# Output weights split again in the second pass, pieces kept for two units, and forms moved to another SBUF offset

## The chip, the cores and the metric

The kernel runs on one core of a Trainium2 chip. The metric is the device time of one execution in microseconds. The profile is one separate execution with the hardware profiler on; it has a time of its own.

## The reference

Inputs: q, k, v of 4 batches x 8 heads x 576 positions x 64; four expert weights w1 (512 x 1024) and w2 (1024 x 512); a dense layer w_in (512 x 2048) and w_out (2048 x 512), which arrive as float64. Everything is computed in float32.

```python
q_s = softmax(q, axis=-1);  k_s = softmax(k, axis=positions)
kv  = einsum('bhsd,bhse->bhde', k_s, v)
x   = einsum('bhsd,bhde->bhse', q_s, kv)        # -> 2304 tokens x 512
p   = domain_probs / (domain_probs.sum(-1) + 1e-9)
y   = sum_e p[:, e] * (relu(x @ w1[e]) @ w2[e]) # 4 experts, 1024 wide
h   = y @ w_in;  out = (h / (1 + exp(-1.702 h))) @ w_out   # 2048 wide
```

## The kernel before, in words

**Precision.** Each large matmul is done in three products of 32-bit "float32r" parts: an operand is split into a high part (a copy on ScalarE, ACT, that rounds) and a low part (the rest, by a subtraction). High x high, high x low and low x high are summed in PSUM.

**Tiling.** The 2304 tokens are three groups, each of two equal halves: group 0 (2 x 512), group 1 (2 x 256) and group 2 (2 x 384). The two layers (experts: "moe", then dense: "ffn") are cut into units of 256 hidden columns: 16 for moe, 8 for ffn. A unit's first product (`mm1`, L842) uses Strassen's seven block products, six matmuls each, so 42 matmuls a step, whose moving operands are the "forms": blocks b11, b21, b12, b22 of x and their sums t1 to t4, each with a high and a low tile (`blocks`, L575). A 512-wide matmul reads 512 columns of a form. The second product (`mm2`, L936) is a 128-token tile at a time, six matmuls of 512 columns: stationary the hidden activations h_hi and h_lo, moving the output weights W2.

**Passes.** SBUF does not hold the forms of all groups, so each layer is passed over twice: first pass with group 0 (one step a unit), second pass with groups 1 and 2 (two steps a unit). In the moe layer the first 3 units (AHEAD) are run before the Strassen forms are there, as plain halves of group 0: steps "L" of units 0, 1, 2 and then "R" of units 0, 1, 2, four products of six matmuls each (`turns`, L674). Each of those six has an index m of its own, 0 to 5 (NPLAIN); `insts` lists all indices.

**Weights.** For each m the pieces of w1 (tag "w1", ring of 10 tiles) and of w2 (tag "w2", ring of 4, halves w20 and w21 of 512 KB with high and low part) are made from raw tiles (`load_w`, ring of 3): a copy on ACT (`hi_w1`, `hi_w2`) and a subtraction on GpSimd (POOL) (`lo_w1`, `lo_w2`). What comes again later is stored to DRAM (`store_part`, L707, in the start through `first_stores`) and read back then in place of being made (`new_part`, L692; `again`, L688). That holds for w1 pieces and w2 halves alike.

**Order.** All engine queues are in order, and the order is the program's. The start (`START`, L1114) is written out by hand: attention of batches 0 and 1 and steps 0 to 5. From step 6 a planner `step` (L1067) issues five stages a step: matmuls and evictions as `STAGES` (L923) says, then the pieces of the next unit's w1 (`prepare`), then w2 (stages 1 and 3, L1098), loads, one deferred transposition to the next layer's input, and some background "turns" (`pump`). In stage 1 stand the rest of the previous step's output tiles (REST), in stage 4 the first half of the next (TILES). The background is first the attention of batches 2 and 3 (`attend2`, L406, two turns a stage; the list of turns is at L543, an empty string is a turn with nothing; a new head enters each eight turns), then the decoding of float64 weights (`decode`, L792, 1.25 turns a stage: five VectorE instructions and more, one on POOL, for each of 32 tiles).

**Lines that the change touches.** `kg`/`kgm` (L483) transpose a column maximum on TensorE and make a diagonal `dg` on VectorE (DVE); `ks` (L489) multiplies it on TensorE, `ksv` subtracts. `xf` (L533) copies an attention result out of PSUM on ACT into `xo` and `put_x` (L633) sends it to DRAM from the SyncE (SP) queue. `to_x2` (L649) transposes a finished moe tile, copies it to `xt` (on DVE where the ffn layer runs already, else on ACT) and sends it from ACT; `xo` and `xt` share a ring of two. `total` (L955) adds a tile into `acc`; the first unit of a pass writes it, for ffn by a copy on ACT. `edge` (L1149) is a tile at the top end of SBUF that nothing reads; the forms of groups 0 and 2 lie below it. With 56 elements all of these tiles begin at 1792 modulo 2048 bytes of a partition; W2, raw tiles, h_hi and h_lo, `acc` and group 1's forms begin at 288 modulo 2048 (w1's pieces too).

Of the kernel before, what the change touches and what calls it, by code (L numbers as in the profile page):

```python
# [8 lines left out]
F32 = mybir.dt.float32  # L9
# [13 lines left out]
def tile_linear_attention_moe_gelu(  # L23
# [32 lines left out]
    P = 128  # L56
# [349 lines left out]
    def attend2(b, j, c0, nc_, keys, live):  # L406
# [109 lines left out]
        def group(g):  # L516
            def t(_):
                y["qT", g] = t_("qT", [P, W])
                y["t", g] = bk(f"t{g}", [P, W])
                for c in range(GS):  # L520
                    T.transpose(
                        y["t", g][:, c * SP : (c + 1) * SP],
                        y["qn"][:, g * GS + c].rearrange("p h d -> p (h d)"), ident[:SP, :SP],
                    )

            def qT(_):
                A.copy(y["qT", g], y["t", g])

            def px(_):
                y["px", g] = bk(f"px{g}", [P, W])  # L530
                T.matmul(y["px", g], kvbd[:, j, :], y["qT", g], start=True, stop=True)  # L531

            def xf(eng):  # L533
                put_x(j, b * S + (c0 + g * GS) * SP, W, y["px", g], A, None)

            for fn in (t, qT, px, xf):
                ops[fn.__name__ + str(g)] = fn
# [288 lines left out]

    acc = {}
    x2 = []  # L830
    def mm(ps, w, x, start, stop):
        (wh, wl), (xh, xl) = w, x
# [9 lines left out]
    def mm1(g, i, m, ho):  # L842
# [92 lines left out]

    def mm2(g, i, lt, m, ho):  # L936

        kind, e, f, pas, first, last = units[g]
# [6 lines left out]
        def product(_=None):  # L945
            y["ps"] = ps = pools["pso", "p"].tile([P, DM], F32, tag="o", name=f"po{g}_{ti}")
            n = 0
            for ft in range(FT):
                hh, hl = h_hi[:, ft, s], h_lo[:, ft, s]
                wh, wl = W2[m, ft]  # L950
                for a, b in ((hh, wh), (hh, wl), (hl, wh)):
                    T.matmul(ps, a, b, start=(n == 0), stop=(n == 3 * FT - 1))  # L952
                    n += 1

        def total(_=None):  # L955
            ps = y["ps"]
# [110 lines left out]
    def step(k_, tiles, before):  # L1067
# [61 lines left out]
        Lb21u:b0@V oa21:1 Lb21v:b0@V a2:s0 rc:2 c2:s0 km:1_0 ra:s0 la21:2@G a2:s1 km:1_2 rc:s0 ra:6 kg:1_0 la:s0 c2:s1  # L1129
        ra:s1 kgm:1_0 kg:1_2 lc:s0 rc:s1 ow21:1 la:s1 kgm:1_2 y0:s0 kdg:1_2 y1:s0 lc:s1 z0:s0 kdg:1_0 k:1_1 z1:s0  # L1130
        oa21:2 +s1:6 ks:1_0 q:1_0 ks:1_2 ksv:1_0 y2:s0 q:1_2 km:1_1 +s3:6 ke:1_0 +s2:6 q:1_1 y3:s0 z2:s0 +s4:6 ksv:1_2
        y1:s1 z3:s0 v:1_3 qm:1_0 ke:1_2 qm:1_2 oa11:0 z1:s1 qs:1_0@G pk:1_2 qm:1_1 oa11:1 qs:1_2@G qe:1_0 pk:1_0
        oa22:1 rz:1_2 rr:1_2 bd0:1_2 bd1:1_2@A qu:1_0 qs:1_1@G oa12:1 ha12:2 kg:1_1 qe:1_2 y0:s1 rz:1_0 kgm:1_1 rr:1_0
        q:1_3 ha22:2 bd0:1_0 qu:1_2 la12:2@G bd1:1_0@A qe:1_1 pk:1_3 ow20:0 la22:2@G z0:s1 qu:1_1 qp:1_2 qp:1_0 qr:1_2
        rc:6 qr:1_0 qn:1_2@G rz:1_3 qm:1_3 a1:s2 rr:1_3 bd0:1_3 c1:s2 bd1:1_3@A kdg:1_1 qp:1_1 oa12:0 qs:1_3@V t1:1_2
        qT1:1_2@A qr:1_1 ow21:0 qe:1_3 ks:1_1 a2:s2 ksv:1_1 qn:1_1@G ra:s2 px1:1_2 la:s2 ke:1_1 oa22:2 xf1:1_2@V
        t0:1_2 pk:1_1 qu:1_3 oa11:2 qT0:1_2@V ow20:1 wh0:2 t0:1_1 qp:1_3 qn:1_0@V px0:1_2 wh1:2 qT0:1_1@A qr:1_3
        wl1:2@G rz:1_1 xf0:1_2@A rr:1_1 c2:s2 bd1:1_1@V rc:s2 oa21:0 bd0:1_1 lc:s2 t1:1_0 qn:1_3@G t0:1_0 qT1:1_0@A
        px0:1_1 oa12:2 qT0:1_0@A px1:1_0 xf0:1_1@V px0:1_0 xf1:1_0@A wl0:2@V t0:1_3 xf0:1_0@V qT0:1_3@A ha11:3 t1:1_3
        t1:1_1 qT1:1_3@V px0:1_3 ha21:3 qT1:1_1@V px1:1_3 xf0:1_3@V ha12:3 px1:1_1 xf1:1_3@A y2:s1 xf1:1_1@V ow21:2  # L1140
        open Hb12:b0 y3:s1 z2:s1 Lb12:b0@V ha22:3 y0:s2 ow20:2 z3:s1 Hb22:b0 y1:s2 z0:s2 Lb22:b0@V wh0:3 wh1:3 ha11:4
        y2:s2 z1:s2 y3:s2 z2:s2 ha21:4 z3:s2 a1:s3 c1:s3 St1:b0@V Ht1:b0 ha12:4 ha22:4 a2:s3 Lt1:b0@G c2:s3 ra:s3
        la:s3 rc:s3 St2:b0@V lc:s3 wh0:4 wh1:4 ha11:5 ha21:5 a1:s4 c1:s4 Ht2:b0 y0:s3 y1:s3 Lt2:b0@G z0:s3 y2:s3 z1:s3
        a2:s4 ra:s4 la:s4 c2:s4 rc:s4 lc:s4 y3:s3 z2:s3 z3:s3 ha11:6 hs4:6 la11:6@V ls4:6@G ha12:5 ha22:5 wh0:5 wh1:5
        a1:s5 c1:s5 St3:b0@V Ht3:b0 y0:s4 a2:s5 ha22:6 la22:6@G y1:s4 z0:s4 ra:s5 Lt3:b0@V la:s5 z1:s4 c2:s5 rc:s5
        lc:s5 y2:s4 ha12:6 hs2:6 la12:6@V y3:s4 z2:s4 hs3:6 ls2:6@V z3:s4 ls3:6@V hs1:6 ls1:6@G St4:b0@G
# [32 lines left out]
    for m in range(NSTART + 1):  # L1179
# [97 lines left out]
```

## Time and profile before

| | us |
|---|---|
| median of 3 runs | 1230.19 (1230.03 to 1230.43) |
| the profiled execution's own time | 1235.11 |
| its span, first to last instruction | 1233.3 |
| TensorE (PE) matmul busy | 1209.0 (98%) |
| DVE busy | 850.4 (69%) |
| ACT busy | 464.7 (38%) |
| POOL busy | 358.7 (29%) |
| DMA | 225.86 MB, 16 engines busy about 56% |

PE is busy nearly everywhere, but matmuls overlap: a 512-column matmul is shown with 0.39 us and the next starts 0.23 us later. So PE's time is read from start to start, or from how long a run of matmuls takes in the chain of work, and not from its busy share. The granted clock is full (2.4 GHz) but for two short stretches, mean 0.995.

### The profile page before, as it was taken

What the parts mean: (1) busy time and instruction counts of PE and PEld (TensorE: products, weight loads), DVE (VectorE), ACT (ScalarE), POOL (GpSimd) and SP (SyncE); (2) the same over time, 40 slices, a digit from 0 to 9 for tenths busy, and PEclk for the clock granted to TensorE, in tenths of its full rate; (3) what the DMA queues carried; (4) which work ended last, traced back from release to release, by engine and by line L of the source; (5) the groups of instructions that cost most, each with busy time, mean ns of one, the idle gap of its engine ahead of it and who ended that gap; (6) DMA issues with size and microseconds to landing.
All of it is one profiled execution on the core that took longest, in us unless ns stands there. A gap on an engine that the chain in (4) does not pass through costs nothing.

```text
span 1233.3 us, 17497 instructions
## 1 busy us (share of the span) xinstructions
PE 1209.0 (98%) x6276; PEld 1043.9 (85%) x6276; DVE 850.4 (69%) x1416; ACT 464.7 (38%) x1010; POOL 358.7 (29%) x389
## 2 busy tenths in 40 slices
PE   8999899999999999999999999999999999999998
PEld 7878688887888899899899889898788889899997
DVE  7875778767567759998999975577355774454554
ACT  5544345433434352222122222145645544333332
POOL 4424657554553001111112331025454500000000
PEclk9999899999999999999999999999999999999999
DMA  8884966664566366666566632535655655334323
GB/s 199 250 303 141 324 210 203 204 230 149 198 217 226 105 198 213 212 209 211 194 194 221 202 110 69 196 121 186 232 203 213 228 170 161 111 107 122 108 92 86
DMA packets 134423, 225.86 MB, mean 183 GB/s; under 512 B 30400, under 2 KB 62144, under 8 KB 133696
## 3 DMA queue, kind: packets, MB, share of 16 engines
q1 hardware_dynamic: 124832, 220.02, 55.2%
q10 hardware_dynamic: 9504, 4.72, 1.3%
q8 instruction: 50, 0.82, 0.3%
q14 instruction: 37, 0.30, 0.1%
HBM read 137.40 MB, written 87.29 MB: 182 GB/s over the span
## 4 chain that ended last, share of the span: by engine, by line
PE 86%; DVE 9%; DMA 4%; ACT 1%; issue 1%; SPq 0%; POOL 0%; ACTq 0%; DVEq 0%
PE po L952 43%; PE px L836 21%; PE pz L836 10%; PE py L836 5%; DVE acc L964 2%; DVE h_lo L885 2%; DMA w64o<-in_moe_w_out 1%; PE pk L506 1%; PE p L378 1%; DMA x_ffn<-xt 1%; PE ca_R L836 1%; PE cc_R L836 1%; DMA q<-in_q 1%; DVE dso L803 1%; PE px L531 1%
## 5 line engine op out<-in xcount | busy, mean ns | idle before, releaser
L952 PE MATMUL po<-w,h_hi 128*128 128x512 f32 x1728 | 538.4, 393 | 2.4 <-DVE xt L110 2.0
L952 PEld LDWEIGHTS po<-w,h_hi 128*128 128x128 f32 x1728 | 320.8, 189 | 65.2 <-DVE xt L110 2.9
L952 PE MATMUL po<-w,h_lo 128*128 128x512 f32 x864 | 337.7, 391 | 3.2 <-DVE h_lo L885 3.2
L964 DVE SCALAR_TENSOR_TENSOR acc<-po,pr,acc 128x512 f32<-128x512 f32 x270 | 194.6, 745 | 70.1 <-PE po L952 69.7
L952 PEld LDWEIGHTS po<-w,h_lo 128*128 128x128 f32 x864 | 162.8, 188 | 39.4 <-DVE h_lo L885 4.5
L110 ACT COPY u<-px 128x384 f32<-128x384 f32 (+2 forms) x138 | 65.3, 473 | 237.7 <-PE px L836 230.3
L973 DVE TENSOR_TENSOR acc<-po,acc 128x512 f32<-128x512 f32 x126 | 85.7, 689 | 58.5 <-PE po L952 57.4
L866 DVE TENSOR_TENSOR u<-pz,u 128x384 f32<-128x384 f32 (+2 forms) x138 | 75.4, 546 | 52.9 <-ACT u L110 52.1
L774 POOL TENSOR_TENSOR s<-s,s 128x256 fp32r<-128x256 f32 x94 | 80.1, 860 | 74.2 <-ACT s L768 59.7
L787 POOL TENSOR_TENSOR w<-rc,w 128x512 fp32r<-128x512 f32 x46 | 60.4, 1314 | 86.6 <-ACT w L781 71.2
L774 POOL TENSOR_TENSOR a<-ra,a 128x256 fp32r<-128x256 f32 x69 | 53.4, 774 | 90.0 <-ACT a L768 80.0
L879 ACT ACTIVATE h_hi<-px 128x256 fp32r<-128x256 f32 (+2 forms) x45 | 21.8, 484 | 144.3 <-PE px L836 144.2
L885 DVE SCALAR_TENSOR_TENSOR h_lo<-u,h_hi 128x256 fp32r<-128x256 f32 (+2 forms) x90 | 63.7, 732 | 12.5 <-ACT h_hi L879 12.3
L823 POOL TENSOR_TENSOR doi<-doi,dti 128x512 f32<-128x512 f32 x16 | 21.0, 1312 | 161.1 <-DVE doi L820 155.0
L762 POOL TENSOR_TENSOR s<-ra 128x256 f32<-128x256 f32 x48 | 40.5, 844 | 75.8 <-DMA ra<-wi 49.8
L866 DVE TENSOR_TENSOR p<-py,p 128x384 f32<-128x384 f32 (+2 forms) x69 | 37.8, 548 | 33.6 <-PE py L836 30.1
L781 ACT CAST w<-rc 128x512 fp32r<-128x512 f32 x48 | 29.6, 620 | 72.2 <-PE po L952 71.5
L879 ACT ACTIVATE h_hi<-u 128x256 fp32r<-128x256 f32 (+2 forms) x90 | 46.3, 515 | 16.0 <-DVE u L866 16.0
L823 POOL TENSOR_TENSOR doo<-doo,dto 128x512 f32<-128x512 f32 x16 | 21.3, 1330 | 103.7 <-DVE doo L820 91.6
L110 ACT COPY p<-px 128x384 f32<-128x384 f32 (+2 forms) x69 | 32.9, 477 | 37.7 <-PE px L836 37.5
L768 ACT CAST s<-s 128x256 fp32r<-128x256 f32 x96 | 36.8, 404 | 24.0 <-POOL s L762 17.1
L889 DVE TENSOR_TENSOR h_lo<-sc,h_hi 128x512 fp32r<-128x512 f32 (+2 forms) x24 | 13.4, 559 | 44.3 <-ACT h_hi L881 44.3
(312 smaller groups left out, 2470.2 us busy)
## 6 DMA issues: line engine op xcount, KB each, us to landing
w<-k_w SPq DMA_DIRECT2D x54, 512.0 KB, 4.5
k_w<-w SPq DMA_DIRECT2D x48, 512.0 KB, 5.1
a<-k_a SPq DMA_DIRECT2D x84, 256.0 KB, 2.8
k_s<-s SPq DMA_DIRECT2D x84, 256.0 KB, 5.2
s<-k_s SPq DMA_DIRECT2D x84, 256.0 KB, 3.3
k_a<-a SPq DMA_DIRECT2D x75, 256.0 KB, 5.2
ra<-in_moe_w SPq DMA_DIRECT2D x19, 512.0 KB, 4.3
rc<-in_moe_w SPq DMA_DIRECT2D x16, 512.0 KB, 6.1
```

Source lines behind the costliest of these rows:

```text
L110: (eng.copy if eng is A else eng.tensor_copy)(o, i)
L762: G.tensor_tensor(out=o, in0=block_w(m, l), in1=block_w(m, r), op=op)
L774: eng.tensor_tensor(out=lo, in0=block_w(m, x), in1=hi.bitcast(F32), op=ALU.subtract)
L787: eng.tensor_tensor(out=lo, in0=raw[m, 1][:, c, :], in1=hi.bitcast(F32), op=ALU.subtract)
L823: G.tensor_tensor(out=o, in0=o, in1=t.bitcast(F32), op=ALU.add)
L836: T.matmul(ps, a[:, kk, :], b[:, kk, :], start=(start and n == 0), stop=(stop and n == 5), skip_group_check=True,)
L866: return lambda _: V.tensor_tensor(out=y[o], in0=y[ps], in1=y[o], op=ALU.add)
L879: A.activation(hi, y[c], AF.Relu)
L885: V.scalar_tensor_tensor(out=lo, in0=y[c], scalar=0.0, in1=hi.bitcast(F32), op0=ALU.max, op1=ALU.subtract)
L952: T.matmul(ps, a, b, start=(n == 0), stop=(n == 3 * FT - 1))
L964: V.scalar_tensor_tensor(out=acc[ti], in0=ps, scalar=pe, in1=acc[ti], op0=ALU.mult, op1=ALU.add)
L973: V.tensor_tensor(out=acc[ti], in0=ps, in1=acc[ti], op=ALU.add)
```

## The change

1. **W2 in the second passes.** Halves of w2 are no longer stored and read back; in the second pass they are loaded raw and split again (ACT copy, POOL subtraction). Only unit 0's, at m = 5, come from DRAM. In `step` they are made in stages 2 and 3, not 1 and 3.
2. **Two units held.** The R halves run in the order 1, 2, 0. Units 1 and 2 use the w1 and w2 pieces of their L halves (`HOME`: m = 3 uses m = 1's, m = 4 uses m = 2's). What the first unit of a tile is, is told by a set `begun`. `START` loses their loads and some stores, and gets m = 5's loads earlier.
3. **Queues.** Attention results of batches 2 and 3 are sent from ACT's queue. `xt` is always copied on ACT; ffn's first `acc` is copied on DVE.
4. **Turns.** One more empty turn before `ks ksv` in `attend2`.
5. **`edge`** has 432 elements: the forms of groups 0 and 2 lie 1504 bytes lower, at 288 modulo 2048.

```diff
-                put_x(j, b * S + (c0 + g * GS) * SP, W, y["px", g], A, None)
+                put_x(j, b * S + (c0 + g * GS) * SP, W, y["px", g], A, None, A)
...
-        turns = ["km", "qm qs", "", "", "kg kgm", "qe", "", "ks ksv", "qu qn", "ke", "", "", "pk", "", "bd"]
+        turns = ["km", "qm qs", "", "", "kg kgm", "qe", "", "", "ks ksv", "qu qn", "ke", "", "", "pk", "", "bd"]
...
-                S_.dma_start(out=x_d["moe", i][:, j, d - g0 : d - g0 + m], in_=o[:, d - t0 : d - t0 + m])
+                by.dma_start(out=x_d["moe", i][:, j, d - g0 : d - g0 + m], in_=o[:, d - t0 : d - t0 + m])
...
-            copy(V if stage[1] else A, o, pt.rearrange("p k t -> p (k t)"))
+            copy(A, o, pt.rearrange("p k t -> p (k t)"))
...
-    turns = [(g, "L") for g in range(AHEAD)] + [(g, "R") for g in range(AHEAD)]
+    turns = [(g, "L") for g in range(AHEAD)] + [(g, "R") for g in (*range(1, AHEAD), 0)]
+    HOME = {AHEAD + n: 1 + n for n in range(AHEAD - 1)}
...
-        names = (PLAIN if m < NPLAIN else STRASSEN) + ("w20", "w21")
+        if m in HOME:
+            continue
+        names = PLAIN if m < NPLAIN else STRASSEN
         again.update({(m, x): (u, x) in had for x in names})
+        again.update({(m, x): m == NPLAIN - 1 for x in ("w20", "w21")})
...
-                    mm(y["c" + x], W1[m, f"a{ft + 1}{kh + 1}"], X[0, b], kh == 0, kh == 1)
+                    mm(y["c" + x], W1[HOME.get(m, m), f"a{ft + 1}{kh + 1}"], X[0, b], kh == 0, kh == 1)
...
-                wh, wl = W2[m, ft]
+                wh, wl = W2[HOME.get(m, m), ft]
...
+            first = (kind, ti) not in begun
+            begun.add((kind, ti))
...
             if first:
-                A.copy(acc[ti], ps)
+                V.tensor_copy(acc[ti], ps)
...
-                if s in (1, 3) and (m, s // 2) not in W2:
-                    hi_w2(m, s // 2)
-                    lo_w2(m, s // 2, G)
+                if s in (2, 3) and (m, s - 2) not in W2:
+                    hi_w2(m, s - 2)
+                    lo_w2(m, s - 2, G)
...
-    pools["edge", "p"].tile([P, 56], F32, name="edge")
+    pools["edge", "p"].tile([P, 432], F32, name="edge")
```

## Rows read from the trace of the kernel before

**Rows 1.** The page, part 4: the chain that ended last, by engine.

```profile
PE 86%; DVE 9%; DMA 4%; ACT 1%; issue 1%; SPq 0%; POOL 0%; ACTq 0%; DVEq 0%
```

**Rows 2.** The chain in order of time: start us, us, what.

```profile
137.03 8.00 PE po L952 x24
...
295.77 4.34 PE px L836 x12
...
334.84 5.46 PE po L952 x24
340.30 2.80 PE px L836 x12
```

**Rows 3.** Timeline of PE, second pass: start us, us, instruction (first of six each).

```profile
464.43 0.34 PE L836 MATMUL px<-t3hmoe,s 128*128 128x384 f32 x1
...
465.47 0.28 PE L836 MATMUL px<-b11hmoe,a 128*128 128x256 f32 x1
...
466.18 0.28 PE L836 MATMUL py<-b21hmoe,a 128*128 128x256 f32 x1
```

**Rows 4.** Waits of PE: who waited for whom, us, times, longest us.

```profile
PE pb L491 <- DVE dg L487: 4.7, 1, 4.7
PE po L952 <- DVE h_lo L885: 3.2, 2, 1.6
PE po L952 <- DVE xt L110: 2.0, 1, 2.0
PE pk L506 <- DVE acc L964: 1.7, 1, 1.7
...
PE pz L836 <- DVE u L866: 1.2, 1, 1.2
```

**Rows 5.** Stretches: us, busy by engine (instructions), granted clock, DMA share, GB/s.

```profile
136.60:142.20 5.60, 5.60 (x15) 4.44 (x15) 4.60 (x6) 3.02 (x8) 5.60 (x7) 0.50 1.02 390
...
500.00:550.00 50.00, 50.00 (x275) 45.06 (x275) 48.62 (x91) 11.19 (x27) 7.88 (x6) 1.00 0.66 202
550.00:600.00 50.00, 50.00 (x279) 45.04 (x277) 44.65 (x84) 10.55 (x26) 6.60 (x6) 1.00 0.65 210
600.00:650.00 50.00, 48.45 (x269) 43.79 (x269) 48.35 (x91) 10.89 (x27) 9.31 (x7) 1.00 0.59 195
650.00:700.00 50.00, 50.00 (x278) 45.18 (x277) 46.76 (x85) 12.45 (x32) 12.66 (x12) 1.00 0.64 211
700.00:745.00 45.00, 42.21 (x235) 37.83 (x234) 35.98 (x58) 11.03 (x29) 15.48 (x17) 1.00 0.35 117
```

**Rows 6.** Timeline of DVE: start us, us, instruction, [idle before].

```profile
134.30 1.93 DVE L487 TENSOR_SCALAR dg<-ident,gm 128x128 f32<-128x128 f32 x1
...
285.81 7.04 DVE L885 SCALAR_TENSOR_TENSOR h_lo<-u,h_hi 128x512 fp32r<-128x512 f32 x1 [0.27 <-ACT h_hi L879]
...
571.58 1.32 DVE L803 TENSOR_SCALAR dsi<-w64i 128x512 int32<-128x512 int32 x1
...
583.90 0.43 DVE L803 TENSOR_SCALAR dso<-w64o 128x512 int32<-128x512 int32 x1 [3.96 <-DMA w64o<-in_moe_w_out]
...
869.33 0.69 DVE L110 COPY xt<-pt 128x512 f32<-128x512 f32 x1 [3.72 <-DMA x_ffn<-xt]
```

**Rows 7.** Timeline of POOL: first and last of the eight that run on end.

```profile
285.07 1.79 POOL L466 TENSOR_TENSOR qn<-q,qu 96x768 f32<-96x768 f32 x1 [0.55 <-DVE qu L462]
...
291.56 0.74 POOL L774 TENSOR_TENSOR s<-s,s 128x256 fp32r<-128x256 f32 x1
```

**Rows 8.** The page, part 5: the two instructions that make a half of W2.

```profile
L787 POOL TENSOR_TENSOR w<-rc,w 128x512 fp32r<-128x512 f32 x46 | 60.4, 1314 | 86.6 <-ACT w L781 71.2
...
L781 ACT CAST w<-rc 128x512 fp32r<-128x512 f32 x48 | 29.6, 620 | 72.2 <-PE po L952 71.5
```

**Rows 9.** The page, part 6: DMA issues, count, KB each, us to landing.

```profile
w<-k_w SPq DMA_DIRECT2D x54, 512.0 KB, 4.5
```

**Rows 10.** Waits of the SP queue at the sending of attention results.

```profile
SPq L646 <- ACT xo L110: 49.3, 11, 12.9
```

More of the change, by code (lines that the diff above doesn't have):

```diff
@@ L631, in forms, with put_x @@
         then()
-    def put_x(j, t0, w, src, eng, first):
+    def put_x(j, t0, w, src, eng, first, by=S_):
         d, o = t0, None
@@ L723, in put_away @@
             stores.pop(0)[1]()
-    stage = [0, False]
+    stage = [0]
     def put_old():
@@ L825, in decode @@
         yield
-    acc = {}
+    acc, begun = {}, set()
     x2 = []
@@ L936, in mm2 @@
     def mm2(g, i, lt, m, ho):
-        kind, e, f, pas, first, last = units[g]
+        kind, e, f, pas, _, last = units[g]
         t0, n = SPANS[i]
@@ L1073, in step @@
         ops = mm1(g, i, m, places[k_])
-        stage[1] = units[g][0] == "ffn"
         st = STAGES[units[g][0]] if k_ + 1 < len(steps) else LAST
@@ L1128, in tile_linear_attention_moe_gelu @@
         px0:0_3 c1:s1 wl1:1@V xf0:0_3@A k:1_0 Hb21u:b0 a1:s1 ha11:2 la22:1@V a1:s0 Hb21v:b0 k:1_2 la11:2@V ha21:2
[L1129 to L1146, printed above, removed]
+        Lb21u:b0@V Lb21v:b0@V a2:s0 rc:2 c2:s0 km:1_0 ra:s0 la21:2@G a2:s1 km:1_2 rc:s0 ra:6 kg:1_0 la:s0 c2:s1 ra:s1
@@ new lines, in tile_linear_attention_moe_gelu @@
+        kgm:1_0 kg:1_2 lc:s0 rc:s1 la:s1 kgm:1_2 y0:s0 kdg:1_2 y1:s0 lc:s1 z0:s0 kdg:1_0 k:1_1 z1:s0 +s1:6 ks:1_0
+        q:1_0 ks:1_2 ksv:1_0 y2:s0 q:1_2 km:1_1 +s3:6 ke:1_0 +s2:6 q:1_1 y3:s0 z2:s0 +s4:6 ksv:1_2 y1:s1 z3:s0 v:1_3
+        qm:1_0 ke:1_2 qm:1_2 oa11:0 z1:s1 qs:1_0@G pk:1_2 qm:1_1 oa11:1 qs:1_2@G qe:1_0 pk:1_0 oa22:1 rz:1_2 rr:1_2
+        bd0:1_2 bd1:1_2@A qu:1_0 qs:1_1@G oa12:1 ha12:2 kg:1_1 qe:1_2 y0:s1 rz:1_0 kgm:1_1 rr:1_0 q:1_3 ha22:2 bd0:1_0
+        qu:1_2 la12:2@G bd1:1_0@A qe:1_1 pk:1_3 ow20:0 la22:2@G z0:s1 qu:1_1 qp:1_2 qp:1_0 qr:1_2 rc:6 qr:1_0 qn:1_2@G
@@ new lines, in tile_linear_attention_moe_gelu @@
+        rz:1_3 qm:1_3 a1:s2 rr:1_3 bd0:1_3 c1:s2 bd1:1_3@A kdg:1_1 qp:1_1 oa12:0 qs:1_3@V t1:1_2 qT1:1_2@A qr:1_1
+        ow21:0 qe:1_3 ks:1_1 a2:s2 ksv:1_1 qn:1_1@G ra:s2 px1:1_2 la:s2 ke:1_1 oa22:2 xf1:1_2@V t0:1_2 pk:1_1 qu:1_3
+        oa11:2 qT0:1_2@V wh0:2 t0:1_1 qp:1_3 qn:1_0@V px0:1_2 wh1:2 qT0:1_1@A qr:1_3 wl1:2@G rz:1_1 xf0:1_2@A rr:1_1
+        c2:s2 bd1:1_1@V rc:s2 oa21:0 bd0:1_1 lc:s2 t1:1_0 qn:1_3@G t0:1_0 qT1:1_0@A px0:1_1 oa12:2 qT0:1_0@A px1:1_0
+        xf0:1_1@V px0:1_0 xf1:1_0@A wl0:2@V t0:1_3 xf0:1_0@V qT0:1_3@A t1:1_3 t1:1_1 qT1:1_3@V px0:1_3 qT1:1_1@V
@@ new lines, in tile_linear_attention_moe_gelu @@
+        px1:1_3 xf0:1_3@V px1:1_1 xf1:1_3@A y2:s1 xf1:1_1@V ha11:5 ha21:5 open Hb12:b0 y3:s1 z2:s1 Lb12:b0@V y0:s2
+        z3:s1 Hb22:b0 y1:s2 z0:s2 Lb22:b0@V y2:s2 z1:s2 y3:s2 z2:s2 z3:s2 a1:s3 c1:s3 St1:b0@V Ht1:b0 a2:s3 Lt1:b0@G
+        c2:s3 ha12:5 ha22:5 ra:s3 la:s3 rc:s3 St2:b0@V lc:s3 a1:s4 c1:s4 Ht2:b0 y0:s3 y1:s3 Lt2:b0@G z0:s3 y2:s3 z1:s3
+        a2:s4 ra:s4 la:s4 c2:s4 rc:s4 lc:s4 y3:s3 z2:s3 z3:s3 wh0:5 wh1:5 ha11:6 hs4:6 la11:6@V ls4:6@G a1:s5 c1:s5
+        St3:b0@V Ht3:b0 y0:s4 a2:s5 ha22:6 la22:6@G y1:s4 z0:s4 ra:s5 Lt3:b0@V la:s5 z1:s4 c2:s5 rc:s5 lc:s5 y2:s4
@@ L1147, in tile_linear_attention_moe_gelu @@
+        ha12:6 hs2:6 la12:6@V y3:s4 z2:s4 hs3:6 ls2:6@V z3:s4 ls3:6@V hs1:6 ls1:6@G St4:b0@G
     """
     open_pool("edge", bufs=1, side="right")
-    pools["edge", "p"].tile([P, 56], F32, name="edge")
+    pools["edge", "p"].tile([P, 432], F32, name="edge")
     open_pool("xp0", bufs=2, side="right")
@@ L1185, in tile_linear_attention_moe_gelu @@
             new["l" + x] = lambda e, m=m, x=x: lo_w1(m, x, e or G)
-            new["o" + x] = lambda _, m=m, x=x: first_stores.pop((m, x))()
+            new["o" + x] = lambda _, m=m, x=x: first_stores.pop((m, x), lambda: None)()
         for c in range(FT):
@@ L1189, in tile_linear_attention_moe_gelu @@
             new[f"wl{c}"] = lambda e, m=m, c=c: lo_w2(m, c, e or G)
-            new[f"ow2{c}"] = lambda _, m=m, c=c: first_stores.pop((m, f"w2{c}"))()
+            new[f"ow2{c}"] = lambda _, m=m, c=c: first_stores.pop((m, f"w2{c}"), lambda: None)()
         add(m, new)
```

## The prediction

> **What bounds the kernel now.** I read the chain of waits first: 86% of it is PE [rows 1]. So the time is PE's matmuls, one after the other, plus the few places where PE stands still, and an edit counts only by what it does to one of the two. Work taken off DMA, ACT, POOL or SP is worth nothing by itself.
>
> The second view is the rate of the matmuls. 24 of 512 columns whose moving operand is W2 take 5.46 us, 227.5 ns each; 12 with a form of group 0 take 2.80 us, 233.3 ns each [rows 2]. In the second pass six forms of 384 columns take 1.04 us (173.3 ns each) and six of 256 take 0.71 us (118.3) [rows 3]. 128 columns more are 55 ns, so 512 should be some 228: W2's matmuls keep to that line and group 0's forms lie 5.8 ns above it.
>
> The third is PE's waits. In the body of the kernel they are five: 4.7 for `dg`, 1.7 for `acc` before a `pk`, 3.2 for h_lo in two places, 1.2 for `u`, 2.0 for `xt` [rows 4]. All name DVE, though DVE is busy only 69% over the span: the average hides stretches in which it is full. Two of the stalls cost twice, since the clock falls behind them. After the first the granted clock is 0.50, the 1.2 GHz level, for some 5 us [rows 5], and 24 matmuls take 8.00 us for 5.46; after the second 12 take 4.34 for 2.80 [rows 2]. Before both falls PE had stood.
>
> Behind these stalls is POOL. While eight POOL instructions run on end from 285.07 to 292.30 [rows 7], one DVE subtraction of two SBUF operands, begun at 285.81, ends at 292.85: of the 7.04 us for two of them nearly 6 are waiting [rows 6]. `dg` has 1.93 us for a 128x128 scaling; a decode step shows 1.32 and the same operation elsewhere 0.43 [rows 6]. So POOL work is not free: it can hold DVE, and DVE holds PE.
>
> The Trainium skill ("SBUF — State Buffer", section "SBUF: two separate sides") says that GpSimd and a VectorE instruction with two SBUF inputs take a port in turn, the loser blocked for the other's whole instruction. The row agrees on the blocking, but 6 us is longer than any one POOL instruction: DVE did not get in between two. By the rule a POOL subtraction more costs DVE at most 1.3 us; by the row a whole run of them. By the rule the slower rival below could cost a step 1.3 us at most, and the sum would stand.
>
> **The change part by part.**
>
> *Forms at 288.* Six steps of 24 matmuls, and 13 + 8 first-pass steps of 42, use 512-column forms: 144 + 882 = 1026. At 5.8 ns each that is 5.9 us. W2 lies at 288 and runs on the lower line in 2592 matmuls; group 0's forms lie at 1792 and don't. What speaks against the offset as cause is that group 2's 384-column forms lie at 1792 too and show nothing. Bounds: 0 to -5.9; a loss is excluded, as W2's matmuls already show how an operand at 288 runs. I take -5.5, some of the 144 lying beside attention's chains in the start.
>
> A rule of the Trainium skill speaks against it: the same page and section says that PE never waits on anyone at its SBUF port, and names no cost of an offset; by it this term would be nil and the sum 5.5 us higher.
>
> *The empty turn before `ks`.* The heads enter every eight turns and two turns make a stage, so `kg` (fifth turn) stays in its stage and `ks` (eighth, now ninth) goes one stage later, for every head. For the first head `ks` stood at the end of stage 3: 12 matmuls (2.8 us) after `kg`, then 4.7 us of waiting. It now comes behind stage 4's 24 output matmuls, 5.5 us more, which cover the wait by 0.8. The wait goes, and the slow clock behind it (8.00 - 5.46 = 2.5 us). Together -7.2. Bounds: 0, if what held DVE comes later too, to -7.2. I take -7.0. Late next is `ke` to `pk`, which loses a stage of distance but keeps one.
>
> *W2 in stages 2 and 3, first passes.* ACT no longer waits for REST before the copy (71.5 us, off PE's path, and POOL waited behind it [rows 8]); but POOL's 1.31 us now stands right before the stage whose h_lo PE needs next. The `pk` stall arose there: 1.7 + 1.5 us of slow clock = 3.2. Bounds: -3.2 (its POOL run is broken up) to +3.2 (a second such place). With nothing to decide between them I take 0.
>
> *W2 made anew in second passes.* Each unit adds two ACT copies of 0.62 and two POOL subtractions of 1.31 us [rows 8] every 26 us. ACT is a quarter busy there. The cost is in the decode, about 450 to 745 us, where DVE is full: 48.6, 44.7, 48.4 and 46.8 of 50 us [rows 5], idle 11.6 us in 200. The trace has a test of more POOL work: with 7.9 busy us in 50 PE loses nothing, with 12.7 neither, with 15.5 in 45 PE is busy only 42.2 [rows 5]. The change adds some 5 us of POOL per 50: the first stretches come to 13, the last, where units 0 to 2 are split too, to 20. DVE loses about half a POOL instruction for each, an estimate from the 0.9 us lost in the row above and none in others: 10 us in 200 against 11.6 idle. On the other side the 54 reads of 512 KB [rows 9], each of which stood on SP until a ring place came free, are mostly gone, so the decode's own loads land sooner: DVE once stood 3.96 us for one, at 580 [rows 6], and PE's loss of 1.55 in the stretch from 600 [rows 5] comes out of that backlog. Bounds: -4.4, if the h_lo and `u` stalls both go; above, 11 units x 2 x 1.31 = 28.8 us of DVE less its idle time at the same share (11.6 x 286/200 = 16.6): +12. I take +3, nearest to what the 15.5 us row cost. After the decode and in ffn DVE is half busy; 0.5 us for short waits, bounds 0 to 1.
>
> *`xt` on ACT, first `acc` on DVE.* The DVE copy waited 3.72 us for an earlier send to land [rows 6], and PE 2.0 behind the next copy. On ACT the same copy would wait for the same landing, now in front of evictions. With no W2 stores beside it the landing should be sooner. Bounds: -2.0 to +2.0; I take -1.
>
> *Sends from ACT, held units, less DMA.* SP stood 49.3 us for `xo` copies [rows 10], and the loads behind them with it; POOL gets its raw weights sooner. Each send costs ACT its issue, and ACT is not among those that PE waits for in the body [rows 4]. About 41 MB less moves (54 + 48 halves less 24 raw loads, and the held pieces), but no DMA is among PE's waits of the body either. I take 0, bounds -1 to +1.
>
> The sum: -5.5 - 7.0 + 0 + 3 + 0.5 - 1 + 0 = -10.0. The profiled execution (1235.11, 1.8 us more than its span) lies 4.9 above the median of the runs; against its own time the sum gives 1225.1, and I carry the difference to the median: 1230.2 - 10 = 1220.
>
> **The rivals.**
>
> *The offset does nothing.* For it: the 384-column forms. Against: 512 columns at 288 and at 1792 differ by the same 5.8 ns throughout. Then -4.5: 1225.7. The skill's rule on PE's port, above, would give this. Chance 0.22.
>
> *The stall moves.* `ks` is covered by only 0.8 us; if DVE or POOL is later by that much, or the later `ksv` makes `pk` wait, PE stands again and the clock falls. Then -3: 1227. For it: the thin cover; against: seven of eight heads had no wait even with the shorter distance. Chance 0.11.
>
> *POOL's port takes it all (slower).* The W2 subtraction in stage 2 joins stage 3's run, so that one contiguous POOL run holds h_lo past the 2.8 us of matmuls that cover it. One such hit costs 3.2 us; there are 21 first-pass steps with this order. From four hits (12.8 us against the gain of 10) the kernel is slower; six give 1220 + 19 = 1239. For it: the 7.04 us; against: in the 20 other steps of before, with the same POOL work, none costs PE that much. Chance 0.11.
>
> *The decode gets better too.* Loads no longer late, both h_lo stalls and `u` gone: -4.4 for +3, 1212.6. For it: the loss after 600 follows a late load. Against: the later ones come where POOL is fullest. Chance 0.10.
>
> **How the numbers follow.** The forecast has 0.46: 1220, its own range 1214 to 1226. The range over all leaves out half of the slower rival and the low tail: 1211 to 1233. About 0.2% (2.5 us) can be told from no change. Faster: all of 0.46, 0.22 and 0.10, less 0.04 for sums that fall short, and 0.05 of the moved stall: 0.79. Slower: 0.10, nearly all of its rival. Within 0.2%: the other 0.11, mostly the moved stall.
>
> **What would show it.** Forms: 12 matmuls of 512 columns in 2.73 us, not 2.80. Turn: no wait for `dg`, no slow clock near 137. W2: DVE's busy time in the decode up by 2 to 3 us in 50, PE's waits for h_lo and `u` together near 7 us. `xt`: its wait under ACT's name and shorter. Wrong it is if the forms' rate stays, if one of these stalls returns under another name with the clock fall behind it, or if DVE's excess in h_lo grows beyond the decode.

## The result: 1.45% slower

The changed kernel takes 1247.7 us (median of 4 runs, 1245.1 to 1250.5) against 1230.1 for the kernel before: a ratio of 1.0145 [1.0119, 1.0170], 17.6 us slower where 10 us faster was forecast. Its profiled execution took 1246.28 us, 1.4 below its median; that of before lay 4.9 above its own, so the two profiles are only 11 us apart and each part is timed by medians of runs below.

The page of the changed kernel: the chain by engine, and the two groups that grew.

```profile
PE 78%; DVE 15%; DMA 2%; issue 2%; POOL 1%; ACT 1%; SPq 0%; ACTq 0%; POOLq 0%
...
L791 POOL TENSOR_TENSOR w<-rc,w 128x512 fp32r<-128x512 f32 x94 | 133.9, 1425 | 313.4 <-ACT w L785 312.5
...
L889 DVE SCALAR_TENSOR_TENSOR h_lo<-u,h_hi 128x256 fp32r<-128x256 f32 (+2 forms) x90 | 81.4, 933 | 9.7 <-ACT h_hi L883 9.6
```

W2's subtraction runs 94 times for 46 [rows 8], as the diff says. DVE has gone from 9% of the chain [rows 1] to 15%. The chain in order of time (start us, us, what) shows where:

```profile
134.61 4.92 DVE h_lo L889 x2
140.99 3.94 PE px L840 x12
...
186.59 8.55 DVE h_lo L889 x3
...
200.11 3.42 PE px L840 x12
...
227.79 2.72 PE px L840 x12
```

12 group-0 matmuls now take 2.72 us for 2.80 [rows 2]: that part came as forecast. But `h_lo` stands in the chain where it did not, and behind two of its places the same 12 take 3.94 and 3.42 us, at a lower clock. By stretch (us, busy PE, PEld, DVE, ACT, POOL, granted clock, DMA share, GB/s) the mean granted clock is 0.69 and 0.80; both stretches begin at 0.50, the 1.2 GHz level, and end at 1.00:

```profile
140.90:145.00 4.10, 4.10 (x15) 3.23 (x15) 4.10 (x5) 0.62 (x2) 1.88 (x4) 0.69 0.78 235
200.00:203.60 3.60, 3.60 (x15) 2.92 (x15) 0.76 (x2) 0.62 (x2) 0.00 (x0) 0.80 1.02 326
```

PE's waits (who for whom, us, times, longest us):

```profile
PE px L531 <- DVE acc L970: 7.5, 3, 5.0
PE po L956 <- DVE h_lo L889: 6.9, 8, 1.8
PE pb L491 <- DVE acc L970: 3.4, 1, 3.4
PE po L956 <- DVE gm L485: 3.0, 1, 3.0
PE po L956 <- DVE acc L970: 2.0, 1, 2.0
```

The waits for `dg` and `xt` of [rows 4] are gone; the first was predicted, the second was to come back shorter under ACT's name. In their place PE waits for `acc` and `gm`, which are not slow themselves: the 5.0, 3.4 and 3.0 us are waits behind DVE's `h_lo` of 6.37, 3.82 and 3.12 us (at 186.50, 135.72 and 220.03). The largest, read on three engines. DVE (start us, us, instruction):

```profile
182.04 0.94 DVE L494 TENSOR_TENSOR k<-k,pb 96x768 f32<-96x768 f32 x1
182.90 1.55 DVE L474 TENSOR_REDUCE mx<-k 96x128 f32<-96x768 f32 x1
184.37 0.94 DVE L460 TENSOR_REDUCE qu<-q 96x12 f32<-96x768 f32 x1
...
185.69 0.89 DVE L448 TENSOR_REDUCE qm<-q 96x12 f32<-96x768 f32 x1
186.50 6.37 DVE L889 SCALAR_TENSOR_TENSOR h_lo<-u,h_hi 128x512 fp32r<-128x512 f32 x1
```

POOL, the first two and the last of those that run on end, and PE:

```profile
185.85 1.72 POOL L466 TENSOR_TENSOR qn<-q,qu 96x768 f32<-96x768 f32 x1 [1.56 <-DVE qu L462]
187.54 1.47 POOL L451 TENSOR_TENSOR q<-q,qm 96x768 f32<-96x768 f32 x1
...
194.55 1.17 POOL L778 TENSOR_TENSOR s<-s,s 128x256 fp32r<-128x256 f32 x1
```

```profile
195.85 1.33 PE L531 MATMUL px<-qT,kvbd 128*128 128x288 f32 x2 [4.99 <-DVE acc L970]
```

The added turn puts all that follows it in a head's list a turn later. So `k` (`ksv`) now stands in one turn with the next head's `mx`, and `qu qn` in one turn with the next head's `qm qs`. `k`, `mx`, `qu` and `qm` run on DVE one behind the other for 4.5 us. `qn` waits for `qu`, `qs` follows it at once, and the `h_lo` behind `qm`, begun 0.65 us after `qn`, lies 6.37 us in POOL's run, through six of its instructions. PE stands 4.99 us. The same place in a kernel that differs from the one before by the offset alone (e1 below), DVE and then POOL:

```profile
179.53 0.95 DVE L494 TENSOR_TENSOR k<-k,pb 96x768 f32<-96x768 f32 x1
...
181.72 0.94 DVE L460 TENSOR_REDUCE qu<-q 96x12 f32<-96x768 f32 x1
...
183.04 1.48 DVE L474 TENSOR_REDUCE mx<-k 96x128 f32<-96x768 f32 x1
184.45 0.93 DVE L448 TENSOR_REDUCE qm<-q 96x12 f32<-96x768 f32 x1
185.31 1.27 DVE L885 SCALAR_TENSOR_TENSOR h_lo<-u,h_hi 128x512 fp32r<-128x512 f32 x2
```

```profile
183.20 1.73 POOL L466 TENSOR_TENSOR qn<-q,qu 96x768 f32<-96x768 f32 x1 [0.51 <-DVE qu L462]
185.46 3.06 POOL L451 TENSOR_TENSOR q<-q,qm 96x768 f32<-96x768 f32 x1 [0.53 <-DVE qm L448]
```

DVE has the same four to do, in another order: `k` early, `qu` before `mx`. So `qn` is over at 184.93, POOL waits for `qm`, and the `h_lo` begins in that gap. This time POOL is the one that is held: its `qs` takes 3.06 us for 1.47.

Which `h_lo` are held is plain from that tile's groups (count: shortest/median/longest ns):

```profile
L889 DVE SCALAR_TENSOR_TENSOR h_lo<-u,h_hi x90: 411/632/6368, 132.7 to 866.7; 128x256 fp32r<-128x256 f32 x32, 128x384 fp32r<-128x384 f32 x32, 128x512 fp32r<-128x512 f32 x26
L889 DVE SCALAR_TENSOR_TENSOR h_lo<-p,h_hi x45: 409/678/3817, 115.7 to 850.5; 128x256 fp32r<-128x256 f32 x16, 128x384 fp32r<-128x384 f32 x16, 128x512 fp32r<-128x512 f32 x13
L889 DVE SCALAR_TENSOR_TENSOR h_lo<-px,h_hi x45: 410/550/692, 130.7 to 861.5; 128x256 fp32r<-128x256 f32 x16, 128x384 fp32r<-128x384 f32 x16, 128x512 fp32r<-128x512 f32 x13
```

The same operation with one operand in PSUM (`px`) never takes more than 0.69 us; with two in SBUF (`u` or `p` and `h_hi`) up to 6.37. The Trainium skill ("SBUF — State Buffer", section "SBUF: two separate sides") names these two kinds apart and agrees. It lets the loser wait for one whole instruction; here it was six on end, and the measurement decides.

In the second passes (columns as above):

```profile
500.00:550.00 50.00, 48.93 (x266) 43.24 (x265) 49.38 (x86) 12.83 (x30) 13.68 (x10) 1.00 0.53 161
550.00:600.00 50.00, 49.28 (x275) 44.46 (x274) 49.38 (x87) 12.85 (x30) 13.02 (x10) 1.00 0.58 179
600.00:650.00 50.00, 47.50 (x258) 42.01 (x257) 49.15 (x82) 12.51 (x29) 13.56 (x10) 1.00 0.58 189
650.00:700.00 50.00, 49.54 (x276) 44.53 (x275) 49.38 (x86) 13.83 (x33) 16.95 (x14) 1.00 0.54 174
700.00:745.00 45.00, 39.68 (x211) 34.29 (x210) 42.41 (x66) 11.20 (x30) 20.36 (x21) 1.00 0.38 129
```

Against [rows 5] POOL has 25.6 us more (77.6 for 51.9) and DVE 15.4 more (239.7 for 224.4): 0.6 us of DVE for each of POOL. DVE is full from 500 to 700, with 2.7 us idle for 11.6, and PE, busy without a gap in three of the five stretches before, has gaps in every one.

To set the kernels side by side I summed PE's loss in each profile: for every matmul the time to the next one's start, less columns / 2.4 GHz and 14 ns (512 columns: 227 ns, what W2's take). In us by stretch of the span:

```
                              0-100  100-320  320-440  440-755  755-   total
before                         23.5     25.2      2.2      5.5   6.0    62.5
offset alone (e1)              22.0     23.6      1.0      5.0   3.5    55.2
all but turn and W2 anew (f1)  21.5     26.7      0.8      6.3   6.8    62.1
all but the turn (e2)          22.9     23.3      1.0     14.3   3.3    64.8
after                          23.1     31.7      0.5     15.0   3.5    73.8
```

Against e1, 8.1 of after's 18.6 us more lie in the stages with attention's heads and 10.0 in the second passes. These are single profiles; a few us of a stretch differ between runs of one kernel.

### The profile page after: what moved, and what is told of

Same layout as the page of the kernel before. It is cut to its first block, busy times and chain, and to the rows that moved or that the text cites. A ratio compares the mean times of both kernels' runs of the same rounds, so it can differ in the third digit from the quotient of the medians.

```text
span 1244.5 us, 17453 instructions
## 1 busy us (share of the span) xinstructions
PE 1209.5 (97%) x6276; PEld 1045.7 (84%) x6276; DVE 901.7 (72%) x1424; ACT 482.7 (39%) x1050; POOL 434.5 (35%) x437
## 4 chain that ended last, share of the span: by engine, by line
PE 78%; DVE 15%; DMA 2%; issue 2%; POOL 1%; ACT 1%; SPq 0%; ACTq 0%; POOLq 0%
PE po L956 39%; PE px L840 18%; PE pz L840 8%; PE py L840 5%; DVE h_lo L889 4%; DVE acc L970 3%; PE pk L506 1%; DVE u L870 1%; DMA ra<-in_moe_w 1%; PE cc_L L840 1%; PE ca_L L840 1%; PE cc_R L840 1%; PE ca_R L840 1%; PE px L531 1%; PE p L378 1%
## 5 line engine op out<-in xcount | busy, mean ns | idle before, releaser
L791 POOL TENSOR_TENSOR w<-rc,w 128x512 fp32r<-128x512 f32 x94 | 133.9, 1425 | 313.4 <-ACT w L785 312.5
L889 DVE SCALAR_TENSOR_TENSOR h_lo<-u,h_hi 128x256 fp32r<-128x256 f32 (+2 forms) x90 | 81.4, 933 | 9.7 <-ACT h_hi L883 9.6
L785 ACT CAST w<-rc 128x512 fp32r<-128x512 f32 x96 | 58.8, 614 | 0.5 <-DMA rc<-in_moe_w 0.5
L893 DVE TENSOR_TENSOR h_lo<-sa,h_hi 128x512 fp32r<-128x512 f32 (+2 forms) x24 | 22.1, 919 | 32.0 <-ACT h_hi L885 31.9
```

What stands on the lines that cost most here:

```text
L785: A.copy(W2[m, c][0], raw[m, 1][:, c, :])
L791: eng.tensor_tensor(out=lo, in0=raw[m, 1][:, c, :], in1=hi.bitcast(F32), op=ALU.subtract)
L889: V.scalar_tensor_tensor(out=lo, in0=y[c], scalar=0.0, in1=hi.bitcast(F32), op0=ALU.max, op1=ALU.subtract)
```

## The experiments

Times are medians; "before" beside them was 1230.1 to 1231.3.

**e1_edge: the offset alone**, on the kernel before.

```diff
-    pools["edge", "p"].tile([P, 56], F32, name="edge")
+    pools["edge", "p"].tile([P, 432], F32, name="edge")
```

> The kernel before with the 432-element edge alone. Theory (offset): 12 group-0 form matmuls take 2.73 us, not 2.80, and the time falls by 4 to 6 us. Rival (the rate comes from something else that the change did to group 0): 2.80 us stays and the time is that of before within 1 us. A second rival: PE gets faster but the same stalls grow by as much, time within 2 us of before at 2.73.

1226.73 us, ratio 0.9967 [0.9954, 0.9980]: -4.0. Its chain in order of time:

```profile
357.25 2.72 PE px L836 x12
```

The forms' rate follows the offset, and nothing else was changed.

**e2_turn: the change without the added turn.**

```diff
-        turns = [..., "qe", "", "", "ks ksv", ...]
+        turns = [..., "qe", "", "ks ksv", ...]
```

> The changed kernel with the old list of turns (ks one turn earlier). Theory (port, turn): the added turn put one head's query normalization and the next head's subtraction of maxima into the same background turn, so POOL runs both on end and holds DVE; without it PE's loss between 130 and 300 us falls from some 24 to at most 14 us and the time by 8 to 14 us. Rival (stage): the second W2 subtraction in stage 2 makes those runs; then the loss stays within 3 us. Both: the decode's loss, 450 to 745, stays near 13 us.

1238.98, 1.0070 [1.0047, 1.0093]. Without the turn the change is 8.7 us faster: the turn costs more than the 7 us that it was to save.

**e3_w2back: the change with W2 stored and read back** (names "w20", "w21" among the stored ones again).

> The changed kernel with the W2 halves stored and read back again from the second occurrence on (held units, turns, stages, sends, offset as changed). Theory (port, decode): PE's loss between 450 and 745 us goes back from some 13 to 5 us and the time falls by 6 to 10 us, with DVE's excess there at 2.5 to 3.5 us in 50 again. Rival (the decode is late for another reason: held units, sends, order of SP): the loss stays above 10 us. The stretch 130 to 300 stays as changed.

1245.81, 1.0113 [1.0095, 1.0131]. PE's loss in the second passes falls from 15.0 to 7.0, but that among the heads rises to 38.0: only 1.9 us come back. With the crowded stage in place the rest can't be read from one such step.

**e4_stage13: W2 in stages 1 and 3 again.**

```diff
-                if s in (2, 3) and (m, s - 2) not in W2:
+                if s in (1, 3) and (m, s // 2) not in W2:
```

> The changed kernel with the W2 halves made in stages 1 and 3 as before. Rival (stage): loss between 130 and 300 us falls by 8 us or more, since the subtraction no longer stands in front of stage 3's run. Theory (turn): it changes by less than 4 us there; in the decode the two POOL subtractions are further apart, so DVE's excess changes by less than 1 us in 50 and the time by less than 4 us in all.

1249.66, 1.0149 [1.0134, 1.0164]: nothing is gained. The place where the prediction put the slower rival is not the one.

**f1_turn_w2back: both undone** (old turns, W2 stored).

> The changed kernel with the old turns and with W2 stored and read back: both suspects undone, the rest (held units, sends from ACT, xt on ACT, stages 2 and 3, offset) as changed. Theory (port: turn and W2 cost, each by itself): the turn gave 8.7 us and W2's decode 8 us of PE's time, so some 1229 to 1233; what then stays above the 1226.7 of before with the edge alone is the cost of the rest, 2 to 6 us. Rival (the attention stretch is chance, any new order loses there): 1238 or more, with 30 us or more of PE's loss before 320.

1234.37, 1.0037 [1.0021, 1.0052]. From here to e2 W2 made anew costs 4.6 us; and 7.6 us over e1 are left for the parts that I had put at nothing.

**f2_qs_later: the change with `qm` and `qs` one turn later.**

```diff
-        turns = ["km", "qm qs", "", "", "kg kgm", ...]
+        turns = ["km", "", "qm qs", "", "kg kgm", ...]
```

> The changed kernel with its added turn kept and the subtraction of the query maxima (qm qs) one turn later, so that it no longer stands in one background turn with the normalization (qn) of the head before. Theory (two POOL instructions on end hold DVE): PE's loss between 100 and 320 us falls from 32 to 24 or less, no wait of 5 us for acc at a px, and the time to 1236 to 1241. Rival (ks later is itself the cost: ksv and qu now stand together in front of h_lo on DVE): the loss stays at 30 us or more and the time within 3 us of the changed kernel.

1237.22, 1.0061 [1.0044, 1.0077]: 10.5 us come back. DVE at the place of the 6.37:

```profile
189.09 1.22 DVE L889 SCALAR_TENSOR_TENSOR h_lo<-u,h_hi 128x512 fp32r<-128x512 f32 x2
190.23 0.68 DVE L889 SCALAR_TENSOR_TENSOR h_lo<-p,h_hi 128x512 fp32r<-128x512 f32 x1
190.83 0.94 DVE L448 TENSOR_REDUCE qm<-q 96x12 f32<-96x768 f32 x1
```

The last three `h_lo` are done in 1.8 us before `qm` starts, and `qs` can only follow that. PE's loss among the heads falls from 31.7 to 23.6. One stall grew all the same: `pb` for `acc`, 7.3 us for 3.4.

**f3_pool: POOL work alone in the second passes.** e1 with one raw load and two POOL subtractions of 128x512 more in each unit there, whose result nothing uses.

> The kernel before with the 432-element edge, W2 stored and read back as before, and beside it a raw load of 512 KB and two POOL subtractions of 128 x 512 a second-pass unit, whose results nothing reads. Theory (POOL's port in the decode): PE's loss between 440 and 755 us goes from 5 to 12 to 15 us, DVE's excess from 3.3 to 6 or more in 50, and the time is 1226.7 plus 7 to 10. Rival (the decode loses through the ACT copies, or since W2 comes later): loss 6 us or less, the time within 2 us of 1226.7.

1239.13, 1.0079 [1.0064, 1.0094]: 12.4 us over e1, and PE's loss from 440 to 755 goes from 5.0 to 16.4. The page's group of the added ones:

```profile
L1110 POOL TENSOR_TENSOR rx<-rx 128x512 f32<-128x512 f32 x48 | 65.5, 1364 | 244.5 <-DMA rx<-wo 174.6 <-DMA rx<-in_moe_w 68.5
```

The added subtractions (65.5 us of POOL), with W2 read back as before, reproduce the loss in the second passes. The run has 24 loads more as well, which it does not separate, so that POOL alone does it is not shown.

**f4_before_qs: a better turn**, e1 with the added turn and `qm qs` a turn later, as in f2.

> The kernel before with the 432-element edge and the changed turn list with qm qs one turn later; nothing else of the change. Theory: the wait for dg goes with its slow clock (4.4 + 2.5 us) and qn and qs don't meet, so 1219 to 1223, faster than both kernels. Rival (the later ks costs by itself): 1227 or more, with new waits between 130 and 300 us.

1223.54 (10 runs), 0.9954 [0.9940, 0.9967]: faster than the kernel before; against e1 3.2 us, with intervals that overlap.

**g1 to g4: the parts that I had put at or near nothing**, each on e1: W2 in stages 2 and 3; sends from ACT; held units; `xt` on ACT with the first `acc` on DVE. The edit of g2:

```diff
-                S_.dma_start(out=x_d["moe", i][:, j, d - g0 : d - g0 + m], ...)
+                by.dma_start(out=x_d["moe", i][:, j, d - g0 : d - g0 + m], ...)   # by = A from the heads
```

> The kernel before with the 432-element edge and W2 made in stages 2 and 3, nothing else. Theory (the 7.7 us that stay when turn and W2 are undone come from the subtraction in stage 2, which joins POOL's run): 1230 to 1234, PE's loss between 100 and 320 us 26 or more, DVE's excess there up by 3 us or more. Rival (sends or held units do it): 1226.7 within 2 us.

1227.06, 0.9975 [0.9962, 0.9987]: +0.3 over e1.

> The kernel before with the 432-element edge and the attention results of batches 2 and 3 sent from ACT. Theory (stage 2): 1226.7 within 2 us, as no engine but ACT gets work and PE doesn't wait for ACT. Rival (sends: ACT's issue delays evictions, or POOL gets raw weights at other times and its runs fall elsewhere): 1229 or more, with new waits between 130 and 310 us.

1234.89 (10 runs), 1.0033 [1.0016, 1.0049]: +8.2.

> The kernel before with the 432-element edge and the held units alone (R halves in the order 1, 2, 0, their START; W2 stored and read back, old turns, stages 1 and 3, sends from SP, xt on DVE). Theory: nothing that PE waits for changes, 1226.7 within 2 us. Rival (held units shift the start of the attention of batches 2 and 3 against the planner): 1229 or more.

1227.55, 0.9976 [0.9963, 0.9988]: +0.8.

> The kernel before with the 432-element edge, xt always copied on ACT and ffn's first acc on DVE. My step had -1 us for this (bounds -2 to +2): 1224.7 to 1228.7, with the wait for xt under ACT's name or gone. Rival: ACT stands for the landing in front of evictions and PE loses 3 us or more near 870, 1230 or more.

1225.93, 0.9964 [0.9951, 0.9977]: -0.8.

So f1's 7.6 us are the sends. In the profile of g2 PE loses 6.5 us from 206 to 230 us, in that of e1 1.6. ACT in g2 at this place (an ACTq line is a send):

```profile
207.24 0.82 ACTq L646 DMA_DIRECT2D x_moe<-xo  x2
208.10 0.59 ACT L110 COPY u<-px 128x512 f32<-128x512 f32 x1 [0.89 <-PE px L836]
208.58 0.63 ACT L879 ACTIVATE h_hi<-u 128x512 fp32r<-128x512 f32 x1
209.11 0.62 ACT L879 ACTIVATE h_hi<-p 128x512 fp32r<-128x512 f32 x1
```

DVE and PE in g2:

```profile
209.95 6.60 DVE L885 SCALAR_TENSOR_TENSOR h_lo<-p,h_hi 128x512 fp32r<-128x512 f32 x1
```

```profile
216.77 0.73 PE L952 MATMUL po<-w,h_hi 128*128 128x512 f32 x2 [3.40 <-DVE gm L485]
```

The same place of e1, DVE:

```profile
207.58 2.16 DVE L885 SCALAR_TENSOR_TENSOR h_lo<-u,h_hi 128x512 fp32r<-128x512 f32 x2
209.66 1.22 DVE L885 SCALAR_TENSOR_TENSOR h_lo<-p,h_hi 128x512 fp32r<-128x512 f32 x1
```

The sends keep ACT until 208.06, `u` is copied then and its `h_hi` made after it. PE, POOL and DVE come to this place 0.3 us later than in e1, ACT's copy of `u` 0.6 (208.10 for 207.51): 0.3 of it is the sends. POOL has the same instructions in both kernels from about 206.5 to 216. In e1 DVE's last `h_lo` begins at 209.66 and takes 1.22 us; in g2 at 209.95 and takes 6.60. Against POOL it begins no later: 0.51 us after the same POOL instruction (`s`, at 209.15 and 209.44) in both. What ACT made later against POOL is the `h_lo` before it (208.66 and 209.25). The hold comes with the sends in these two profiles; by which step the last `h_lo` lost its place is not shown.

**h1_after_dve, h2_f4_dve: `qn` and `qs` on DVE** (`(eng or G)` to `(eng or V)` at both lines), in the changed kernel and in f4, to shorten POOL's run.

> The changed kernel with the two attention subtractions and normalizations of batches 2 and 3 (qs and qn, 1.5 to 1.8 us each on POOL) done on DVE; turns, sends, W2 as changed. Theory (POOL's run holds DVE): PE's loss between 100 and 320 us falls from 32 to 22 or less, no h_lo of 3 us or more there, though DVE gets some 15 us more work; the time 1236 to 1241. Rival (the order of turns and sends by itself, or DVE's load): loss 30 us or more, time 1245 or more.

> The kernel before with the 432-element edge, the added turn with qm qs one turn later, and qs and qn on DVE. Theory: the 7 us h_lo near 283 goes as well, so 3 to 5 us less than the 1223.5 without it: 1218 to 1221. Rival (DVE's own 15 us more cost what POOL's runs did): 1223 or more.

1249.44, 1.0150 [1.0116, 1.0184], and 1228.13 (10 runs), 0.9978 [0.9963, 0.9994]: no better, and 4.6 us worse than f4. The long holds are gone in h1 (shortest/median/longest ns), and yet PE's loss among the heads is 34.5 for 31.7:

```profile
L889 DVE SCALAR_TENSOR_TENSOR h_lo<-u,h_hi x90: 411/582/1793, 132.0 to 870.3; 128x256 fp32r<-128x256 f32 x32, 128x384 fp32r<-128x384 f32 x32, 128x512 fp32r<-128x512 f32 x26
```

DVE and PE in h1:

```profile
157.54 0.95 DVE L494 TENSOR_TENSOR k<-k,pb 96x768 f32<-96x768 f32 x1
...
164.78 2.71 DVE L970 SCALAR_TENSOR_TENSOR acc<-po,pr,acc 128x512 f32<-128x512 f32 x4
```

```profile
165.57 0.75 PE L531 MATMUL px<-qT,kvbd 128*128 128x288 f32 x2 [4.00 <-DVE acc L970]
```

Now DVE's own head work, 157.54 to 164.85 without a gap, keeps `acc` from PE, 4.00 us where the changed kernel had waited 1.2; at the place of the 4.99 PE still stands 2.0. In the time of the kernel it makes no difference here which of the two engines has the work: a hold by POOL is one way in which DVE comes late, a full DVE is another.

**i1_after_qs_only, i2_after_km: which half of f2 did it?** The changed kernel with `qs` alone a turn later, and with `km` two turns later and the rest as it was.

```diff
-        turns = ["km", "qm qs", "", "", "kg kgm", ...]
+        turns = ["km", "qm", "qs", "", "kg kgm", ...]     # i1
+        turns = ["", "qm qs", "km", "", "kg kgm", ...]    # i2
```

> The changed kernel with qs alone one turn later, so that POOL's qn and the next head's qs are no longer on end, while DVE's ksv, mx, qu and qm stay in one stage. Theory (POOL's run): PE's loss between 100 and 320 us falls from 32 to 26 or less, the time to 1241 or less. Rival (DVE's burst): 29 us or more, time 1245 or more.

> The changed kernel with km (mx, 1.55 us on DVE) two turns later, so that DVE's burst in the stage of ksv and qu falls from 4.7 to 3.2 us, while qn and qs stay on end on POOL. Rival (DVE's burst): loss falls from 32 to 26 or less, time 1241 or less. Theory (POOL's run): 29 us or more, 1245 or more.

1246.38, 1.0121 [1.0101, 1.0142], and 1245.34, 1.0120 [1.0103, 1.0137]. Neither brings back what f2 did: PE's loss among the heads is 32.7 and 31.1 for 31.7. Parting `qn` from `qs` on POOL is not enough, nor is taking `km` from DVE's burst; by what was expected of them, each run speaks against one of the two mechanisms alone. What in f2 is needed, `qm` off DVE, or that together with `qs` off POOL, stays open.

**h3_f4_xt: the best parts**, f4 with `xt` on ACT.

> The kernel before with the 432-element edge, the added turn with qm qs one turn later, xt on ACT and ffn's first acc on DVE. The last part gave 0.8 us on the edge alone, within its spread: 1222 to 1224 if it adds, 1226 or more if the combination meets a POOL run again.

1223.56, 0.9939 [0.9916, 0.9963] against 1230.7 beside it: the best ratio of all, though not apart from f4's.

**i3_spread: `km` and `qm qs` two turns late each**, the rest as in f4 (there `km` is in its place and `qm qs` one turn late).

> The kernel before with the 432-element edge and the added turn, km two turns later and qm qs two turns later: DVE's burst is split into ksv and qu (2.2 us) and km and qm (2.5 us) in two stages, and qn and qs stand apart. Either mechanism gives 1219 to 1223 here, at or below the 1223.5 of the version with qm qs one turn later; 1226 or more if neither sets the loss.

1229.62 (10 runs), 0.9990 [0.9981, 1.0000]: a miss, 6 us worse than f4. PE's waits in i3 and then in f4:

```profile
PE px L531 <- DVE acc L964: 5.3, 2, 2.7
```

```profile
PE px L531 <- DVE acc L964: 2.6, 1, 2.6
```

Of the two in i3 one is f4's; the other is new. DVE in front of it in i3, and the same two `h_lo` in f4:

```profile
178.74 5.84 DVE L885 SCALAR_TENSOR_TENSOR h_lo<-u,h_hi 128x512 fp32r<-128x512 f32 x2
```

```profile
180.28 1.22 DVE L885 SCALAR_TENSOR_TENSOR h_lo<-u,h_hi 128x512 fp32r<-128x512 f32 x2
```

PE's loss from 180 to 210 us is 7.8 for f4's 2.2, nearly the whole difference. Spreading more is not better here: this order makes a new meeting of `h_lo` and POOL's run.

## Why the prediction was wrong

Step by step the medians go -4.0 (offset, e1), +7.6 (f1 over e1), +4.6 (W2 anew, e2 over f1), +8.7 (turn, after over e2): +16.9 for the 17.6 measured. Such a chain of differences must come near the whole; the check is that g1 to g4, each on e1 by itself, sum to 8.5 for the 7.6. The shares depend on the order: by e3 the turn costs 11.4 (over f1) and W2 anew 1.9. The forecast's -10.0 missed by 27.6, of which the turn is 15.7 and the sends 8.2.

- *The empty turn before `ks`, -7.0: the step that failed most.* It measured +8.7 beside the other parts; alone on the kernel before it was not run. What I said of `dg` held. But I had only `ks` go a stage later, and asked what is late next only for `ke` and `pk`. Everything behind the added turn goes later, and I never asked what it meets there: on DVE `ksv` and `qu` meet the next head's `mx` and `qm`, and on POOL `qn` meets the next head's `qs`. I counted the wait of the moved step alone. "Seven of eight heads had no wait" was read as slack; it was an order that fitted. Moving `qm qs` too brings 10.5 us back (f2), and with that the turn on e1 gives 1223.5 (f4). How much of the cost is POOL's hold and how much DVE's own crowding stays open: without the hold the time is the same (h1).
- *Sends from ACT, 0 within 1: failed too*, +8.2 (g2). I looked whether ACT is among those that PE waits for, and it is not; but DVE waits for ACT's `h_hi`, the sends make that 0.3 us later against POOL, and a `h_lo` near it takes 6.60 us for 1.22. SP's 49.3 us [rows 10] bought nothing.
- *W2 made anew, +3: the right mechanism, too small.* +4.6 by f1 to e2; added POOL work cost 12.4 (f3), just over the upper bound of 12. DVE's own loss was sized about right (10 us in 200 forecast; 8.9 from 500 to 700, 197.3 busy for 188.4). What failed is the cover: I let DVE's idle us count to the last, and PE loses with 2.7 of them left in 200.
- *Forms at 288, -5.5:* -4.0, right in sign and rate (2.72 us for 12), and -5.5 lies within the interval of e1 (-5.7 to -2.5). By the rule of the Trainium skill ("SBUF — State Buffer", section "SBUF: two separate sides") that PE waits on nobody at its port, the term would be nil; e1 decides against it, and that rival falls.
- *`xt`, -1:* -0.8 (g4). *Held units and W2 in stages 2 and 3, 0:* +0.8 and +0.3, each inside what can be told.
- *The slower rival* had the mechanism, a POOL run that holds `h_lo` past its cover, and nearly its price (waits of 3.0 to 5.0 us for 3.2), at a place that does nothing (e4, g1). It had 0.11, and I worked it out for one edit only; the turn, the sends and W2 in the second passes feed the same mechanism elsewhere.

*The stall moves* came true in kind: gone under `dg`, back under `acc` and `gm` with the clock's fall behind it (3.94 and 3.42 for 2.72). Its -3 for the whole change, which is a turn worth nothing in place of -7, was far too small a price. The prediction's "7.04 us for two of them" is one instruction in its row (x1): some 6.4 of it are waiting, so that the hold itself was read too small as well.

## What to carry to other kernels

Before you move a step, write down the order of every engine's work in the stage that it leaves and in the one that it enters; a wait taken away there can come back larger under another name. Where one engine can hold another for a whole run of instructions, no work on a third is off the path until its effect on their order is followed, even where it moves things by 0.3 us. Time each part of a compound change by itself: here the offset, `xt` on ACT and a corrected turn together give a kernel 0.6% faster than the one before; sends from ACT and W2 made anew cost.

## What had not been expected of the hardware

- The place of a matmul's moving operand in SBUF changes its rate: 512 columns take 233 ns at 1792 modulo 2048 bytes and 227 at 288 (e1), while 384 columns take 174 ns at both (before and e1). In all it is worth 4.0 us (e1). Only these two places were measured; why they differ, and whether 2048 is the right measure, is not shown.
- A DVE instruction of two SBUF operands is held over several POOL instructions in a row (6.37 and 6.60 us; 7.04 in [rows 6]), and where it starts first POOL is held instead (`qs` 3.06 us for 1.47). Why it gets in between two of them at 209.66 in e1 and not at 209.95 in g2, begun as long after the same POOL instruction, is not settled.
